# Attention mix on one core: 172 instead of 158 blocks on VectorE, earlier score products for them, the reciprocal product on GpSimd, and other costs in the list

## The chip, the core and the metric

The kernel runs on one core of a Trainium2 chip. The metric is the device time of one execution in microseconds. The core has five engines with instruction streams of their own: TensorE (PE; its weight loads are PEld in the profile), VectorE (DVE), ScalarE (ACT), GpSimd (POOL) and SyncE (SP), which issues the DMAs here. Each executes its instructions in the order written; they wait for each other through semaphores.

## What is computed

Two attention blocks read the same input x (2048 rows, 512 wide, 32 heads of 16). A is full attention over all 2048 keys, B a dilated window of 8 keys two rows apart. A gate mixes the two.

```
g = sigmoid((x * gate_w).sum(-1))
A: p = softmax(q k^T / 4) over 2048 keys;       a = (p v) @ A_wo
B: p = softmax(q . k[s - 2w], w = 0..7);        b = (p v) @ B_wo
out = g * a + (1 - g) * b
```

## The kernel before

**Periods and blocks.** Queries are cut into four chunks of 512. A period `pi` is one chunk with a group of four heads (32 periods, L320); its scores are 16 key tiles of 128 x 4 heads = 64 blocks of 128 x 512. Of every period's blocks, `n_dve[pi]` go to VectorE and the others to ScalarE.

**Blocks on ScalarE.** Blocks are taken in sets of 3 and 2 in turn. For a set, PE makes the score products into one of two PSUM rings (`qk`, L896: one 32-row strip a head, so that products of different heads run together), ScalarE takes the exponential of the whole set into `pT` (`ex`, L902), and PE adds its products with v to the period's accumulator `acc` (`pv`, L924: one 32-column strip a head).

**Blocks on VectorE.** For such a block PE makes an offset product and a score product into a misc bank (`dq`, L964), VectorE computes the exponential as a polynomial in four passes over 128 x 512 (`p1` to `p4`, L971 to L985; tiles `dt` and `pd`), and PE adds it to `acc` (`pv` of `d_group`, L994), for two blocks at a time.

**End of a period.** VectorE transposes `acc` into `accT` (`po1`), takes the reciprocal of the denominators into `rden` and multiplies by it into `ott` (`po2`, L1027), and after two periods transposes `ott` into `oat` (`po3`, L1034). When a chunk is complete, PE multiplies `oat` by the output weights (`wop`), and adds branch B's part (`bwo`).

**Branch B.** Its projections are on PE; its logits, softmax and weighted sums are on GpSimd, tile by tile of 128 rows, in halves of four window places (`logits_half`, L751; `av_half`, L800), with loads of shifted rows by SyncE.

**What sets the order.** Every piece of work is an `Op` (L104) with an engine, a cost `occ`, a latency `lat`, a due time `dl`, and the buffers it takes. `list_schedule` (L128) plans all of them: among the ops that can start about now on an engine it takes the one that is due first. The result is written out as one fixed order for each engine, and the instructions are chained in it (L262). The costs and due times are numbers in the source, so changing one moves instructions on all engines. An op that reads what GpSimd made is planned `slack` later than GpSimd's planned end (L215).

**Filler.** PE's planned work in the last 3.41 us (`SPAN`) is summed; where it is below the share `cover`, the list puts matmuls with a zero weight ahead of the next op (L184 to L199). `zero` (L941) writes them either to a spare misc bank or, adding nothing, to the accumulator of an open period:

```
spots = [(pi, j) for (pi, j), left in todo.items() if 1 <= left < NT]
for _ in range(n if spots else 0):
    pi, j = spots[-1]
    mm(acc_tiles[pi][32 * j:32 * j + 32, :], z32[:], ones_t[:], False, False, tile_position=(0, 32 * j))
```

**PSUM.** Two rings take five of the eight banks; the other three are the misc banks, shared by accumulators, projections and the block products of VectorE.

Of the kernel before, what the change touches and what calls it, by code (L numbers as in the profile page):

```python
# [9 lines left out]
ALU = mybir.AluOpType  # L10
AX = mybir.AxisListType
FP32 = mybir.dt.float32
# [4 lines left out]

CFG = dict(
    set_sizes=(3, 2),
    n_dve=(3,) * 2 + (4,) * 14 + (6,) * 16,  # L20
    dve_tiles=2,
    p_bufs=4,
    pairs=True,
    cover=0.74,
    force=1.0,
    d_slack=2.0,
    d_lead=4.0,
    d_early=5.0,
    pd_bufs=3,
    q_bufs=3,  # L30
    shift=6.0,
    hold=0.3,
    pv_dl=2.2,
    same=2.0,
    step=2,
    early=0.25,
    a_slack=0.6,
    v_slack=0.3,
    g_slack=4.0,
    unit=0.457,  # L40
    t0=18.5,
    b_start=32.0,
    b_space=46.7,
# [4 lines left out]
DH = 16  # L48
# [70 lines left out]


LAT = dict(pe=0.25, dve=0.10, act=0.22, pool=2.5, sp=2.2)
WAVE = lambda n: 0.03 + 0.205 * n
TURN = 0.13
SPAN, COVER, ZERO = 3.41, CFG["cover"], 0.216
AHEAD = dict(pe=0.10, dve=0.12, act=0.25, pool=0.5, sp=0.0)

# [96 lines left out]
def kernel(  # L223
# [12 lines left out]
    cfg = CFG  # L236
# [7 lines left out]
    TPC = QW // 128  # L244
    NBG = S // 32
    BPC = QW // 32
# [4 lines left out]
    work = ctx.enter_context(tc.tile_pool(name="work", bufs=2))  # L251
# [18 lines left out]
    def chain(bi):  # L270
        return chain_on("pe", bi)
# [13 lines left out]
    V = Chained(nc.vector, "dve")  # L285
    A = Chained(nc.scalar, "act")
    G = Chained(nc.gpsimd, "pool")
    SP = Chained(nc.sync, "sp")

    def mm(out, lhsT, rhs, start, stop, **kw):  # L290
        return chain(nc.tensor.matmul(out, lhsT=lhsT, rhs=rhs, start=start, stop=stop, **kw))  # L291

    def mm_ct(out, lhsT, rhs, start, stop):
# [10 lines left out]
    def op(eng, occ, fn, dl, **kw):  # L304
        o = Op(eng, occ, fn, dl, **kw)
        ops.append(o)
        return o
# [13 lines left out]
    NP = len(periods)  # L321
# [5 lines left out]
    n_dve = cfg["n_dve"]  # L327
# [8 lines left out]
    while u < len(units):  # L336
        n = SZ[len(sets) % 2]
# [31 lines left out]
    ott2 = const.tile([128, 2, BPC, 32], BF16, name="ott2")  # L369
# [106 lines left out]
    for sc in range(NC):  # L476
        st = {}
        halves = []
        for half in range(2):
            tag = ("rA", "rB")[half]  # L480
# [34 lines left out]
    o_kc = {}  # L515
    o_selk, o_kc0 = {}, []
# [80 lines left out]
    for h0, h1, pn in ((4, 8, 2), (8, 16, 4), (16, 24, 8), (24, 32, 12)):  # L597
        TB = 512 // ((h1 - h0) * DH)
        for tb in range(0, NT, TB):
            late = tb + TB > NT - NTD  # L600
# [6 lines left out]
    qt_tiles, o_q, q_tok, last_q = {}, {}, {}, [None]  # L607
# [36 lines left out]
    for sc in range(NC):  # L644
        st = {}
# [14 lines left out]
        dl = 32.0 + 2 * sc  # L660
        a = op("pe", 0.9, zc, dl, deps=[o_bw] + o_xt[sc], alloc=[tk], rel=T0 + 4.0)
# [22 lines left out]
    a = op("act", 0.25, zsig, 43.0, deps=[a], use=[tzp])  # L684
# [8 lines left out]
    def b_tile(t):  # L693
# [106 lines left out]
        def av_half(hf):  # L800
# [23 lines left out]
                    if hf:  # L824
                        G.tensor_tensor(out=st["obb"][:, cs], in0=ob[:, cs], in1=prod[:, 0, cs], op=ALU.add)
            return s
        l0 = op("pool", 10.2, logits_half(0), tb + 8, deps=[lk, qa], alloc=[tlg], use=[tks, tqb], name=f"lg{t}")
        l1 = op("pool", 10.2, logits_half(1), tb + 18, deps=[l0], use=[tks, tqb, tlg])
        a = op("dve", 0.45, sm_pre, tb + 19, deps=[l1], use=[tlg])
        a = op("pool", 0.75, sm_sub, tb + 19, deps=[a], use=[tlg], lat=0.9, slack=4.0)  # L830
        a = op("act", 0.45, sm_exp, tb + 18, deps=[a], use=[tlg])
        a = op("dve", 0.85, sm_post, tb + 21, deps=[a], use=[tlg])
        a = op("pool", 0.75, sm_div, tb + 21, deps=[a], use=[tlg], lat=0.9, slack=0.3)
        a0 = op("pool", 9.3, av_half(0), tb + 40, deps=[a, lv], alloc=[tob], use=[tlg, tvs])
        a1 = op("pool", 10.6, av_half(1), tb + 48, deps=[a0], alloc=[tbb], use=[tlg, tvs, tob])
        tk = tok("misc", NB)
        if cb not in obt_tok:
            obt_tok[cb] = tok("obt", 2)
# [47 lines left out]
    for k, us in enumerate(sets):  # L886
        st = {}
        ring = "rA" if k % 2 == 0 else "rB"
        maxn = SZ[k % 2]
        n = len(us)  # L890
        tr_ = tok(ring, 1)
        tp = tok("pT" + ring, cfg["p_bufs"])
        tn = T0 + UNIT * sum(SZ) * (k // 2) + (UNIT * SZ[0] if k % 2 else 0)
        pis = sorted(set(u_[0] for u_ in us))

        def qk(us=us, st=st, ring=ring, maxn=maxn):  # L896
            st["r"] = ps.tile([128, maxn, QW], FP32, tag=ring, bufs=1, name="ring")
            for s_, (pi, t, j) in enumerate(us):
                mm(st["r"][:, s_, :], kt_all[32 * j:32 * j + 32, periods[pi][1], t * 128:(t + 1) * 128],
                   qt_tiles[pi][32 * j:32 * j + 32, :], True, True, tile_position=(32 * j, 0))  # L900

        def ex(us=us, st=st, ring=ring, maxn=maxn, n=n):  # L902
            st["p"] = work.tile([128, maxn, QW], BF16, name="pT", tag="pT" + ring, bufs=cfg["p_bufs"])
            A.activation(out=st["p"][:, 0:n, :], in_=st["r"][:, 0:n, :], func=ACT.Exp, scale=LN2 / BITS)
        kd = [(o_kc[periods[pi][1]] if periods[pi][1] else o_kc0)[t // TPC] for pi, t, j in us]
        a = op("pe", 0.20 + 0.025 * (n - 1), qk, tn - 3.0, rows=True, deps=[o_q[pi] for pi in pis] + kd,
               alloc=[tr_], use=[q_tok[pi] for pi in pis], lat=0.47, after=[last_qk[0]], name=f"qk{k}")
        last_qk[0] = a
        b = op("act", 0.08 + 0.427 * n, ex, tn, deps=[a], alloc=[tp], use=[tr_], name=f"ex{k}")
        pend.append((us, st, tp, b))  # L910
        if cfg["pairs"] and len(pend) < 2 and k + 1 < len(sets):
            continue
        members, pend = pend, []
        for pi in sorted(set(u_[0] for m_ in members for u_ in m_[0])):
            mine = [(m_, s_, t, j) for m_ in members for s_, (p_, t, j) in enumerate(m_[0]) if p_ == pi]
            while mine:
                wave = {}
                for x in mine:
                    wave.setdefault(x[3], x)
                wave = list(wave.values())  # L920
                mine = [x for x in mine if x not in wave]
                from_ = [m_ for m_ in members if any(x[0] is m_ for x in wave)]

                def pv(pi=pi, wave=wave):  # L924
                    for m_, s_, t, j in wave:
                        pv_mm(pi, t, j, m_[1]["p"][:, s_, :], vp_all[:, t])
                first = pi not in o_first
                o = op("pe", 0.205 + 0.015 * len(wave), pv, tn + cfg["pv_dl"],
                       deps=[m_[3] for m_ in from_] + [o_v[(4 * periods[pi][1] + j, t)] for _, _, t, j in wave]
                       + ([] if first else [o_first[pi]]),  # L930
                       alloc=[acc_tok[pi], acc_two[pi]] if first else [],
                       use=[m_[2] for m_ in from_] + ([] if first else [acc_tok[pi], acc_two[pi]]), name=f"pv{k}",
                       sums=[((pi, x[3]), 1, NT) for x in wave])
                if first:
                    o_first[pi] = o
                o_pv[pi].append(o)
                if t_first[pi] < 4:
                    t_first[pi] += sum(1 for _, _, t, j in wave if t == 0)
                    o_t0[pi] = o

    def zero(n, spare):  # L941
        if spare:
            bank[0] = spare.bank
            zp = misc_ps([128, QW])
            for _ in range(n):
                mm(zp[0:32, :], z32[:], ones_t[:], True, True, tile_position=(0, 0))
            return
        spots = [(pi, j) for (pi, j), left in todo.items() if 1 <= left < NT]
        for _ in range(n if spots else 0):
            pi, j = spots[-1]  # L950
            mm(acc_tiles[pi][32 * j:32 * j + 32, :], z32[:], ones_t[:], False, False, tile_position=(0, 32 * j))

    d_last = [None]
# [1 line left out]
    def d_group(pi, gr, lo, hi):  # L955
# [5 lines left out]
        def chain_of(q_, t, j, dl):  # L961
# [20 lines left out]
            def p4():  # L982
                if q_ == 0:
                    st["pd"] = work.tile([128, 2, QW], BF16, name="pd", tag="pd", bufs=cfg["pd_bufs"])
                V.tensor_tensor(out=st["pd"][:, q_, :].bitcast(U16), in0=st["x"][:], in1=st["dt"][:], op=ALU.add)  # L985
            a = op("pe", 0.41, dq, dl - 3.8, rows=True, deps=[o_q[pi], o_kc[i][t // TPC] if i else o_kc0[t // TPC]],
                   after=[d_last[0]], alloc=[tx], use=[q_tok[pi]], rel=lo, lat=0.68, name=f"dq{pi}")
            a = op("dve", 0.70, p1, dl - 2.3, deps=[a], alloc=[td], use=[tx])
            a = op("dve", 0.70, p2, dl - 1.4, deps=[a], use=[td, tx])
# [14 lines left out]
    for pi in range(NP):  # L1004
        gs = [dorder[u_:min(u_ + 2, n_dve[pi])] for u_ in range(0, n_dve[pi], 2)]
        plen = S0[pi + 1] - S0[pi]
        for m, gr in enumerate(gs):
            d0 = S0[pi] - shift(pi)
            d_group(pi, gr, d0 - cfg["d_lead"], d0 + 2.5 + (plen - cfg["d_early"]) * (m + 1) / len(gs))


    oat_tiles, oat_tok, ott_tok, o_oat, o_ott = {}, {}, {}, {}, {}
    for pi, (c_, i) in enumerate(periods):
# [11 lines left out]
            V.transpose(out=st["a"][:].rearrange("p b d -> p (b d)"), in_=acc_tiles[pi][:])  # L1025

        def po2(c_=c_, i=i, st=st):  # L1027
            rden = work.tile([128, BPC], FP32, name="rden", tag="rden", bufs=2)
            V.reciprocal(out=rden[:], in_=st["a"][:, :, DH:DH + 1].rearrange("p b o -> p (b o)"))
            rd_bc = _ap(rden[:], [list(rden[:].ap[0]), [1, BPC], [0, DH]])  # L1030
            g0 = DH * (i % 2)
            V.tensor_tensor(out=ott2[:, c_ % 2, :, g0:g0 + DH], in0=st["a"][:, :, 0:DH], in1=rd_bc, op=ALU.mult)

        def po3(pi=pi, c_=c_, i=i):  # L1034
            if c_ not in oat_tiles:
                oat_tiles[c_] = work.tile([128, NG // 2, QW], BF16, name="oat", tag="oat", bufs=2)
            V.transpose(out=oat_tiles[c_][:, i // 2, :], in_=ott2[:, c_ % 2].rearrange("p b d -> p (b d)"))
        a = op("dve", 0.75, po1, E - 1.0, deps=o_pv[pi], alloc=[ta], use=[acc_tok[pi], acc_two[pi]], slack=cfg["a_slack"])
        o_ott[c_, i] = op("dve", 0.90, po2, E + 4.0, deps=[a], alloc=[to] if i % 2 == 0 else [], use=[ta] + ([to] if i % 2 else []))
        if i % 2:  # L1040
            o_oat[c_, i] = op("dve", 0.74, po3, E + 6.0, deps=[o_ott[c_, i], o_ott[c_, i - 1]] + ([o_oat[c_, i - 2]] if i > 1 else []),
                           alloc=[oat_tok[c_]] if i == 1 else [], use=[to] + ([oat_tok[c_]] if i > 1 else []))
# [122 lines left out]
```

## Time and profile before

| | us |
|---|---|
| runs | 898.36, 899.66, 899.74 (median 899.66) |
| profiled execution | 898.22, span 896.4 |
| first exponential pT starts, last ends | 18.6, 887.6 |
| ScalarE busy | 869.3 |
| PE busy | 788.9 |
| VectorE busy | 679.1 |
| GpSimd busy | 605.9 |
| mean granted clock of PE | 0.981 |

In the rows of the profile, L282 is the helper through which VectorE, ScalarE, GpSimd and SyncE instructions are recorded, and L291 that of the matmuls, so that the tiles' names tell the groups apart: `pT<-ring` are the exponentials, `ring<-qt,kt_all` the score products of ScalarE's blocks, `misc<-ones_t,off` and `misc<-qt,kt_all` the two of a VectorE block, `acc<-pT,vp_all` and `acc<-pd,vp_all` the sums with v, `acc<-ones_t,z` the filler. A row of windows gives, for a stretch from A to B, its length, then busy time and number of instructions of PE, PEld, VectorE, ScalarE and GpSimd, then the granted clock as a share of full speed. Busy times of PE overlap with its pipeline; a matmul of 512 columns shows some 0.38 us, but the next can start earlier.

### The profile page before, as it was taken

The numbers are of one execution on the slowest core, as the hardware profiler recorded it, in microseconds if no ns is written. First come the engines' busy times: TensorE is split into PE (matmuls) and PEld (weight loads), VectorE is DVE, ScalarE is ACT, GpSimd is POOL, SyncE is SP. The second block draws the span as 40 slices with busy tenths as digits, with TensorE's granted clock in tenths as the row PEclk, the third lists the DMA queues.
The fourth block names the chain that finished last, engine by engine and source line by source line (L and its number), as shares of the span: only waits on it lengthen the run. The fifth ranks groups of instructions, "written<-read, shape, count | busy, mean of one in ns | idle before, by whom it ended". The sixth has DMA issues, their size and how long they took to land.

```text
span 896.4 us, 18567 instructions
## 1 busy us (share of the span) xinstructions
PE 788.9 (88%) x7487; PEld 259.5 (29%) x7487; DVE 679.1 (76%) x1095; ACT 869.3 (97%) x782; POOL 605.9 (68%) x577
## 2 busy tenths in 40 slices
PE   9989998888888888898888988988888888889896
PEld 4223332223322233222222322222222222222221
DVE  6567667776768786768578888787879887788875
ACT  5999999999999999999999999999999999999996
POOL 4357849595959895969984597979798977700000
PEclk9999999999999999999999999799999999999978
DMA  9303011111030303020311211030230301000001
GB/s 278 113 2 106 2 61 48 59 48 60 2 106 2 106 2 106 7 101 2 96 36 60 71 48 60 13 95 15 92 107 3 105 1 48 1 1 1 1 13 36
DMA packets 43998, 47.37 MB, mean 53 GB/s; under 512 B 1876, under 2 KB 41348, under 8 KB 43912
## 3 DMA queue, kind: packets, MB, share of 16 engines
q1 hardware_dynamic: 43912, 46.19, 16.0%
q8 instruction: 58, 0.95, 0.4%
q14 instruction: 28, 0.23, 0.1%
HBM read 39.86 MB, written 6.33 MB: 52 GB/s over the span
## 4 chain that ended last, share of the span: by engine, by line
ACT 65%; issue 22%; PE 9%; DVE 1%; POOL 1%; DMA 1%; ACTq 0%; SPq 0%; DVEq 0%
ACT pT L282 64%; PE ring L291 3%; PE acc L291 3%; PE misc_ps L291 2%; ACT lg L282 1%; PE misc L291 1%; POOL prod L282 1%; DMA xld<-in_A_x_dram 1%; PE pxt L487 0%; DVE dt L282 0%; ACTq L1160 0%; DVE kmax_all L282 0%; SPq L282 0%; DVE osb L282 0%; DVE qt L282 0%
## 5 line engine op out<-in xcount | busy, mean ns | idle before, releaser
L282 ACT ACTIVATE pT<-ring 128x1536 bf16<-128x1536 f32 x756 | 860.4, 1420 | 9.7 <-PE ring L291 6.3
L291 PE MATMUL ring<-qt,kt_all 32*128 32x512 bf16 x1890 | 301.5, 385 | 98.2 <-ACT pT L282 92.6
L291 PE MATMUL acc<-pT,vp_all 128*17 128x512 bf16 (+1 forms) x1890 | 260.1, 389 | 0.8 <-DVE vp_all L282 0.5
L282 POOL TENSOR_TENSOR prod<-prod 128x512 f32<-128x512 f32 (+1 forms) x208 | 241.3, 1173 | 6.3
L291 PEld LDWEIGHTS <-kt_all 32*128 32x128 bf16 x2048 | 124.1, 91 | 389.5 <-issue 373.0
L282 POOL TENSOR_TENSOR prod<-ksh,qb 128x512 f32<-128x512 bf16 x128 | 144.5, 1161 | 50.3 <-DMA ksh<-kv_scr 30.9
L282 DVE TENSOR_SCALAR dt<-misc 128x512 f32<-128x512 uint16 x158 | 108.5, 687 | 70.5 <-PE misc L291 68.1
L282 POOL TENSOR_TENSOR prod<-vsh,lg 128x512 f32<-128x512 bf16 x128 | 137.9, 1109 | 2.5
L282 DVE SCALAR_TENSOR_TENSOR dt<-misc,dt 128x512 f32<-128x512 uint16 x158 | 108.8, 688 | 4.6
L282 DVE TENSOR_TENSOR dt<-misc,dt 128x512 f32<-128x512 uint16 x158 | 108.7, 688 | 4.6
L282 DVE TENSOR_TENSOR pd<-misc,dt 128x512 uint16<-128x512 f32 x158 | 108.6, 687 | 4.4
L291 PEld LDWEIGHTS <-vp_all 128*17 128x17 bf16 (+1 forms) x2048 | 55.9, 88 | 127.0 <-issue 115.9
L291 PE MATMUL acc<-ones_t,z 128*32 128x512 bf16 x233 | 85.4, 394 | 0.0
L291 PE MATMUL misc_ps<-xT,wtw 128*32 128x512 bf16 x1024 | 85.4, 383 | 0.0
L291 PE MATMUL misc_ps<-bw,xT 128*32 128x512 bf16 x768 | 66.1, 390 | 0.0
L291 PE MATMUL misc<-ones_t,off 32*128 32x512 bf16 x158 | 60.8, 385 | 0.4 <-DVE accT L282 0.3
L291 PE MATMUL misc<-qt,kt_all 32*128 32x512 bf16 x158 | 60.1, 380 | 0.0
L282 POOL TENSOR_TENSOR lg<-lg,rr 128x256 f32<-128x256 f32 x16 | 10.1, 629 | 57.0 <-DVE rr L282 40.5
L282 POOL TENSOR_TENSOR lg<-lg,mx 128x256 f32<-128x256 f32 x16 | 10.3, 644 | 49.0 <-DVE mx L282 49.0
L291 PEld LDWEIGHTS <-xT 128*32 128x32 bf16 (+1 forms) x1088 | 32.0, 96 | 27.7 <-issue 20.2
L282 DVE TENSOR_SCALAR misc_ps<-misc_ps,magn 128x512 uint32<-128x512 uint32 x32 | 24.1, 754 | 15.2 <-PE misc_ps L291 14.9
L291 PE MATMUL acc<-pd,vp_all 128*17 128x512 bf16 x158 | 34.2, 391 | 0.0
(72 smaller groups left out, 499.0 us busy)
## 6 DMA issues: line engine op xcount, KB each, us to landing
ksh<-kv_scr SPq DMA_DIRECT2D x16, 1024.0 KB, 5.7
vsh<-kv_scr SPq DMA_DIRECT2D x16, 1024.0 KB, 6.1
kv_scr<-kvs SPq DMA_DIRECT2D x16, 256.0 KB, 2.0
xld<-in_A_x_dram SPq DMA_DIRECT2D x4, 512.0 KB, 7.6
out_dram<-osb SPq DMA_DIRECT2D x16, 128.0 KB, 1.7
bw<-in_B_wqkv_dram SPq DMA_DIRECT2D x1, 1536.0 KB
wraw<-in_A_wqkv_dram SPq DMA_DIRECT2D x2, 512.0 KB, 8.7
wv<-in_A_wqkv_dram SPq DMA_DIRECT2D x1, 512.0 KB, 9.0
```

The source lines that it names most:

```text
L282: return chain_on(key, f(*a, **k))
L291: return chain(nc.tensor.matmul(out, lhsT=lhsT, rhs=rhs, start=start, stop=stop, **kw))
```

## The change

Fourteen periods (2 to 15) get 5 instead of 4 blocks on VectorE. `dq` is due 10 us earlier, and the block sums of every period but the last 8 us later (`d_late`). The product with the reciprocal becomes an op of its own on GpSimd, except in the last two periods. The filler goes, where it can, to the column strip of the matmul before it. `cover` falls from 0.74 to 0.68, and the list's costs for PE, ScalarE and GpSimd are replaced; `first` is 0 and has no effect.

```diff
-    n_dve=(3,) * 2 + (4,) * 14 + (6,) * 16,
+    n_dve=(3,) * 2 + (5,) * 14 + (6,) * 16,
-    cover=0.74,
+    cover=0.68,
+    dq_early=10.0,
+    d_late=8.0,
+    first=0.0,
-    unit=0.457,
+    unit=0.461,
...
-WAVE = lambda n: 0.03 + 0.205 * n
-TURN = 0.13
+WAVE = lambda n: 0.01 + 0.205 * n
+TURN = 0.10
...
     def mm(out, lhsT, rhs, start, stop, **kw):
+        strip[0] = kw.get("tile_position", (0, 0))[1] // 32
...
-        l0 = op("pool", 10.2, logits_half(0), ...
-        l1 = op("pool", 10.2, logits_half(1), ...
+        l0 = op("pool", 9.6, logits_half(0), ...
+        l1 = op("pool", 9.6, logits_half(1), ...
...
-        a0 = op("pool", 9.3, av_half(0), ...
-        a1 = op("pool", 10.6, av_half(1), ...
+        a0 = op("pool", 8.8, av_half(0), ...
+        a1 = op("pool", 10.0, av_half(1), ...
...
-        a = op("pe", 0.20 + 0.025 * (n - 1), qk, ...
+        a = op("pe", 0.21 + 0.003 * (n - 1), qk, ...
-        b = op("act", 0.08 + 0.427 * n, ex, ...
+        b = op("act", 0.047 + 0.432 * n, ex, ...
-                o = op("pe", 0.205 + 0.015 * len(wave), pv, tn + cfg["pv_dl"],
+                o = op("pe", 0.207 + 0.003 * len(wave), pv, tn + cfg["pv_dl"] - (cfg["first"] if first else 0.0),
...
-            pi, j = spots[-1]
+            pi, j = max(spots, key=lambda x: (x[1] == strip[0], x[0]))
...
-            a = op("pe", 0.41, dq, dl - 3.8, ...
+            a = op("pe", 0.43, dq, dl - 3.8 - cfg["dq_early"], ...
...
-            d_group(pi, gr, d0 - cfg["d_lead"], d0 + 2.5 + (plen - cfg["d_early"]) * (m + 1) / len(gs))
+            late = cfg["d_late"] if pi < NP - 1 else 0.0
+            d_group(pi, gr, d0 - cfg["d_lead"], d0 + 2.5 + late + (plen - cfg["d_early"]) * (m + 1) / len(gs))
...
+        def po2m(pi=pi, c_=c_, i=i, st=st):
...
+            (V if pi >= NP - 2 else G).tensor_tensor(out=ott2[:, c_ % 2, :, g0:g0 + DH], in0=st["a"][:, :, 0:DH], in1=rd_bc, op=ALU.mult)
...
-        o_ott[c_, i] = op("dve", 0.90, po2, E + 4.0, ...
+        a = op("dve", 0.26, po2, E + 0.2, deps=[a], use=[ta])
+        if pi >= NP - 2:
+            o_ott[c_, i] = op("dve", 0.45, po2m, E + 0.3, ...
+        else:
+            o_ott[c_, i] = op("pool", 0.75, po2m, E + 1.5, deps=[a], lat=0.95, slack=2.0, ...
```

More of the change, by code (lines that the diff above doesn't have):

```diff
@@ L288 @@
     SP = Chained(nc.sync, "sp")
+    strip = [0]
     def mm(out, lhsT, rhs, start, stop, **kw):
+        strip[0] = kw.get("tile_position", (0, 0))[1] // 32
         return chain(nc.tensor.matmul(out, lhsT=lhsT, rhs=rhs, start=start, stop=stop, **kw))
@@ L826, in av_half @@
             return s
-        l0 = op("pool", 10.2, logits_half(0), tb + 8, deps=[lk, qa], alloc=[tlg], use=[tks, tqb], name=f"lg{t}")
-        l1 = op("pool", 10.2, logits_half(1), tb + 18, deps=[l0], use=[tks, tqb, tlg])
+        l0 = op("pool", 9.6, logits_half(0), tb + 8, deps=[lk, qa], alloc=[tlg], use=[tks, tqb], name=f"lg{t}")
+        l1 = op("pool", 9.6, logits_half(1), tb + 18, deps=[l0], use=[tks, tqb, tlg])
         a = op("dve", 0.45, sm_pre, tb + 19, deps=[l1], use=[tlg])
@@ L833, in b_tile @@
         a = op("pool", 0.75, sm_div, tb + 21, deps=[a], use=[tlg], lat=0.9, slack=0.3)
-        a0 = op("pool", 9.3, av_half(0), tb + 40, deps=[a, lv], alloc=[tob], use=[tlg, tvs])
-        a1 = op("pool", 10.6, av_half(1), tb + 48, deps=[a0], alloc=[tbb], use=[tlg, tvs, tob])
+        a0 = op("pool", 8.8, av_half(0), tb + 40, deps=[a, lv], alloc=[tob], use=[tlg, tvs])
+        a1 = op("pool", 10.0, av_half(1), tb + 48, deps=[a0], alloc=[tbb], use=[tlg, tvs, tob])
         tk = tok("misc", NB)
@@ L905 @@
         kd = [(o_kc[periods[pi][1]] if periods[pi][1] else o_kc0)[t // TPC] for pi, t, j in us]
-        a = op("pe", 0.20 + 0.025 * (n - 1), qk, tn - 3.0, rows=True, deps=[o_q[pi] for pi in pis] + kd,
+        a = op("pe", 0.21 + 0.003 * (n - 1), qk, tn - 3.0, rows=True, deps=[o_q[pi] for pi in pis] + kd,
                alloc=[tr_], use=[q_tok[pi] for pi in pis], lat=0.47, after=[last_qk[0]], name=f"qk{k}")
         last_qk[0] = a
-        b = op("act", 0.08 + 0.427 * n, ex, tn, deps=[a], alloc=[tp], use=[tr_], name=f"ex{k}")
+        b = op("act", 0.047 + 0.432 * n, ex, tn, deps=[a], alloc=[tp], use=[tr_], name=f"ex{k}")
         pend.append((us, st, tp, b))
@@ L985, in p4 @@
                 V.tensor_tensor(out=st["pd"][:, q_, :].bitcast(U16), in0=st["x"][:], in1=st["dt"][:], op=ALU.add)
-            a = op("pe", 0.41, dq, dl - 3.8, rows=True, deps=[o_q[pi], o_kc[i][t // TPC] if i else o_kc0[t // TPC]],
+            a = op("pe", 0.43, dq, dl - 3.8 - cfg["dq_early"], rows=True, deps=[o_q[pi], o_kc[i][t // TPC] if i else o_kc0[t // TPC]],
                    after=[d_last[0]], alloc=[tx], use=[q_tok[pi]], rel=lo, lat=0.68, name=f"dq{pi}")
@@ L1027, in po2 @@
         def po2(c_=c_, i=i, st=st):
-            rden = work.tile([128, BPC], FP32, name="rden", tag="rden", bufs=2)
-            V.reciprocal(out=rden[:], in_=st["a"][:, :, DH:DH + 1].rearrange("p b o -> p (b o)"))
+            st["rden"] = work.tile([128, BPC], FP32, name="rden", tag="rden", bufs=2)
+            V.reciprocal(out=st["rden"][:], in_=st["a"][:, :, DH:DH + 1].rearrange("p b o -> p (b o)"))
+        def po2m(pi=pi, c_=c_, i=i, st=st):
+            rden = st["rden"]
             rd_bc = _ap(rden[:], [list(rden[:].ap[0]), [1, BPC], [0, DH]])
             g0 = DH * (i % 2)
-            V.tensor_tensor(out=ott2[:, c_ % 2, :, g0:g0 + DH], in0=st["a"][:, :, 0:DH], in1=rd_bc, op=ALU.mult)
+            (V if pi >= NP - 2 else G).tensor_tensor(out=ott2[:, c_ % 2, :, g0:g0 + DH], in0=st["a"][:, :, 0:DH], in1=rd_bc, op=ALU.mult)
         def po3(pi=pi, c_=c_, i=i):
@@ L1038 @@
         a = op("dve", 0.75, po1, E - 1.0, deps=o_pv[pi], alloc=[ta], use=[acc_tok[pi], acc_two[pi]], slack=cfg["a_slack"])
-        o_ott[c_, i] = op("dve", 0.90, po2, E + 4.0, deps=[a], alloc=[to] if i % 2 == 0 else [], use=[ta] + ([to] if i % 2 else []))
+        a = op("dve", 0.26, po2, E + 0.2, deps=[a], use=[ta])
+        if pi >= NP - 2:
+            o_ott[c_, i] = op("dve", 0.45, po2m, E + 0.3, deps=[a], alloc=[to] if i % 2 == 0 else [], use=[ta] + ([to] if i % 2 else []))
+        else:
+            o_ott[c_, i] = op("pool", 0.75, po2m, E + 1.5, deps=[a], lat=0.95, slack=2.0, alloc=[to] if i % 2 == 0 else [], use=[ta] + ([to] if i % 2 else []))
         if i % 2:
```

## The prediction

> **What bounds the kernel now.** I read the page's busy times and costliest groups first, then the waits of ScalarE, then windows around them. In the group line, "860.4, 1420" is busy time and mean of one, "9.7" the idle time before.
>
> ```profile
> PE 788.9 (88%) x7487; PEld 259.5 (29%) x7487; DVE 679.1 (76%) x1095; ACT 869.3 (97%) x782; POOL 605.9 (68%) x577
> ...
> L282 ACT ACTIVATE pT<-ring 128x1536 bf16<-128x1536 f32 x756 | 860.4, 1420 | 9.7 <-PE ring L291 6.3
> ```
>
> In the waits of ScalarE the columns are total, times and longest, in us:
>
> ```profile
> ACT pT L282 <- PE ring L291: 6.3, 10, 1.7
> ACT pT L282 <- PE acc L291: 2.8, 3, 1.1
> ACT pT L282 <- PE misc L291: 0.4, 1, 0.4
> ```
>
> ScalarE's exponentials are the clock of this kernel: 860.4 us of the 896.4 us span, and the chain of waits gives ACT 65%. The first starts at 18.6 us, the last ends at 887.6 us; between them ScalarE stops for 9.5 us less the 1.7 us before the first, so 7.8 us. All of it is waiting for TensorE (PE). The windows tell the two kinds apart (length, then busy PE, PEld, DVE, ACT, POOL, then the granted clock):
>
> ```profile
> 491.80:495.20 3.40, 3.05 (x34) 1.03 (x33) 3.18 (x6) 2.53 (x3) 0.10 (x1) 1.00 0.20 77
> 565.82:569.23 3.41, 2.18 (x20) 0.71 (x20) 3.27 (x7) 3.41 (x4) 3.33 (x4) 1.00 0.02 5
> 569.23:579.47 10.24, 10.24 (x60) 1.84 (x58) 7.27 (x12) 8.27 (x8) 10.08 (x10) 0.50 0.00 0
> 620.43:623.85 3.42, 2.55 (x21) 0.87 (x19) 3.35 (x8) 3.42 (x5) 3.42 (x4) 1.00 0.00 0
> 859.37:862.78 3.41, 2.58 (x18) 0.97 (x18) 3.27 (x7) 3.41 (x5) 0.00 (x0) 1.00 0.00 0
> 862.78:873.02 10.24, 10.24 (x54) 2.01 (x53) 6.76 (x11) 8.75 (x8) 0.00 (x0) 0.50 0.04 14
> 541.90:545.30 3.40, 2.42 (x22) 0.75 (x18) 3.30 (x7) 3.40 (x4) 0.00 (x0) 1.00 0.75 255
> ```
>
> First kind: four stretches (from 569, 624, 709 and 863 us; 10.24, 3.41, 3.41 and 10.24 us long) with the granted clock at 0.50. PE is then busy throughout and ScalarE starves. They hold the waits for "ring" other than the first and the one for "misc": 6.3 - 1.7 + 0.4 = 5.0 us. Each follows a stretch of 3.41 us in which PE was busy for only 2.2 to 2.6 us; 542 us shows that not every such stretch (2.42 us) brings one. Second kind: three stops at full clock (494.0, 502.1, 814.0 us; 0.87, 0.87, 1.09 us), together the 2.8 us for "acc", where the list put too much other PE work between two score sets.
>
> **Part by part.**
>
> *Fourteen blocks leave ScalarE.* n_dve sums to 2x3 + 14x4 + 16x6 = 158 before and 2x3 + 14x5 + 16x6 = 172 after, so ScalarE gets 1876 blocks instead of 1890, in 751 exponentials instead of 756. At 860.4 / 1890 = 0.455 us a block that is 14 x 0.455 = **6.4 us off the engine that bounds**. Nothing hides ScalarE's time, so it comes off whole.
>
> *VectorE takes them.* Each costs four passes of 0.688 us: 14 x 4 x 0.688 = +38.5 us. The reciprocal product leaves it in 30 of 32 periods:
>
> ```profile
> L282 DVE TENSOR_TENSOR ott<-accT,rden x32: 424/566/1423, 55.2 to 889.1; 128x256 bf16<-128x256 f32 x32
> ```
>
> ```profile
> 300.00:500.00 200.00, 177.07 (x1773) 59.36 (x1769) 146.47 (x231) 199.13 (x180) 153.43 (x146) 1.00 0.18 58
> 500.00:700.00 200.00, 175.35 (x1563) 53.67 (x1561) 167.36 (x262) 196.52 (x178) 174.66 (x165) 0.97 0.18 56
> ```
>
> The first row is minimum, median and maximum in ns; the windows' third busy time is VectorE's. The group's 22.8 us less two of 0.425 at the end makes -21.9 us. The additional blocks all lie in periods 2 to 15, about 74 to 458 us. There VectorE is 146.5 / 200 = 73% busy; 38.5 us over 384 add 10 points, the products leaving (about 13 of 0.88 us) take 3 off: 80%. From 500 to 700 us it already runs at 84% with six blocks a period, and every ScalarE stop there is accounted for above without it. So I cost VectorE at nothing; the cover is this idle fifth, and without it each late block sum holds PE's queue, and the score sets behind it.
>
> *The product on GpSimd* is not in the trace. Nearest row: its 128x256 product lg<-lg,rr, 0.629 us; 30 x 0.63 = 19 us on an engine with 290 us idle, which ends its own work at about 784 us: nothing on the path. A far bound is its slowest single step, 1.5 us, which still makes only 45 us. What can cost is the wait: its reader on VectorE, the oat transpose (L1037), and all block passes queued behind that. In the built order the transpose stands 2 to 23 VectorE instructions after the reciprocal, as against 2 to 5 before, so mostly past the product's time. I take 0; the high bound is rival 3.
>
> *Score products ahead of the passes* (due times 10 us earlier) change when dq is issued on PE, not its cost, 0.43 us. VectorE waits 68.1 us for this product now, 81 times; less of that makes the 80% easier. An earlier dq holds one of three misc banks longer; PE's waits for VectorE at these tiles are 0.5 us in all today. I take 0.
>
> *Filler matmuls.* The list uses 211 after, 240 before. What matters is whether they add PE time:
>
> ```profile
> 492.27 0.39 PE L291 MATMUL acc<-ones_t,z 128*32 128x512 bf16 x1
> 492.28 0.39 PE L291 MATMUL acc<-pd,vp_all 128*17 128x512 bf16 x2
> 492.50 0.38 PE L291 MATMUL acc<-ones_t,z 128*32 128x512 bf16 x1
> ```
>
> The first filler shares its time with the block sums, which start 10 ns later; the second starts 220 ns after. Before, 76 of the 240 stand right behind a matmul of another column strip and so can run beside it; after, since the strip of the last matmul is preferred, 5 of 211. Fillers that add time go from 164 to 206. With 14 x 0.43 us more block products, the streaming time of all matmuls counted from the order (0.216 us a step, different strips together; both as the starts above are apart) rises from 558 to 573 us. Stretches of three score sets (about 3.4 us, as long as those above) with less than half of streaming fall from 13 to 8. I scale the half-clock cost by that: 5.0 x 8/13 = 3.1, so **-1.9 us**. Bounds: -5.0 (no drop left) and +5.0 (twice as many, if the lower count of fillers decides).
>
> The Trainium skill, "TensorE: Matmul & The Clock Gate", section "HAM oscillation — how this bites in real kernels", says that the clock halves after PE-idle gaps above some 3.4 us. This trace disagrees: the half clock follows stretches with PE busy for 2.2 to 2.6 of 3.41 us. By that rule the fillers decide nothing, and the sum would be that of rival 1.
>
> *New crowding.* Full-clock stops appear in the order before: PE work between two score sets (priced under rival 2) exceeds ScalarE's 1.13 us by 1.03, 0.81 and 1.23 us at the three places (stops 0.87, 0.87, 1.09), while three lone excesses of 0.8 cost nothing. The order after has one big excess, 2.3 us, near set 412: eight bwo products, two of dq, nine sums, sixteen wop products, five sums in a row. I price it at 2.3 and its neighbour of 0.8 at 0.5: 2.8, as before, so 0. Bounds -0.8 (the big one alone, reduced by the ring's lead to 2.0) and +1.
>
> **Sum:** -6.4 - 1.9 + 0 = -8.3 us. The profiled execution took 898.2 us (span 896.4 and 1.8 around it), so it would be 889.9; it lies 1.4 us under the median 899.66, to which I apply the sum: **891.4 us**. Own range: -6.4 - 5.0 - 0.8 to -6.4 + 1, or 887.5 to 894.3 (to 899.3 with drops doubled).
>
> **Rivals.**
>
> 1. *Fillers don't matter, the drops stay.* For: 542 us had a stretch as thin as the others without a drop; the drops depend on where stretches fall. Only ScalarE's share counts: 899.66 - 6.4 = 893.3 us.
>
> 2. *Crowding on PE eats the gain.* PE work in the order (the streaming steps and 0.10 us for each change between row and column tiling, as score set to sum starts 0.31 us apart) rises by 13.5 us (703 to 716.5) against a shorter ScalarE time; stretches of two score sets with more PE than ScalarE work go from 55 to 81. Against: most of the 55 cost nothing. If each of the 26 costs 0.25 us, 6.5 us return: 897.9 us, about no change.
>
> 3. *Slower: VectorE blocked behind the GpSimd product.* GpSimd runs in order, and half a logits tile is 4 x 1.16 + 3 x 1.27 + 0.61 + 0.43 = 9.5 us in one piece. A product that arrives inside one waits 4.8 us on average. At six of the 15 transposes fed by GpSimd only 3 to 6 VectorE instructions (about 3 us of cover) lie between; the rest, 1.8 us, stops the passes. If no lead of the passes over the sums absorbs it, PE and ScalarE stop as long: 6 x 1.8 = 10.8 us, giving 902.2 us. It decides from 8.3 / 6 = 1.4 us for each. Against: VectorE never waited noticeably for GpSimd at mx<-lg (0.0 us idle before it), which the same list places; and planned halves (9.6 us) are no shorter than the measured 9.5.
>
> **Numbers.** Forecast 0.57, rival 1 0.22, rival 2 0.08, rival 3 0.13. About 0.2% (1.8 us) can be told from no change. Faster: the first two and a third of rival 2, 0.81; within 0.2%: 0.06; slower 0.13. The range runs from 886.5 (all drops gone and stops at full clock shrunk) to 899.5 us, which leaves out rival 3 and little else.
>
> **What would show it.** ScalarE's pT group at about 854 us in 751; VectorE busy near 696, GpSimd near 625. Right: few or short half-clock slices, one ScalarE stop of 2 us near 470 us, none on VectorE's account. Wrong: half-clock time above the present 27 us, waits of VectorE's oat for GpSimd with PE's acc waits behind them, or many small ring waits at full clock.

## The result, and the profile after

| | before | changed |
|---|---|---|
| median of four runs, us | 899.13 | 890.01 (888.93 to 891.62) |
| ratio | | 0.9901, interval 0.9883 to 0.9918 |
| profiled execution, us (span) | 898.22 (896.4) | 891.62 (889.8) |

The kernel is 9.1 us faster at the median; 8.3 was forecast, to 891.4 us. Beside the experiments below the changed kernel was timed once more: 890.01 against 897.38 (ratio 0.9926, interval 0.9897 to 0.9954). The medians in this document leave out five runs counted as slow (a_oldstrip 904.6 and 907.4 us, a_dveprod 901.9 and 1094.6, g_h02_c71 902.3; the one of 1094.6 us had a mean granted clock of 0.552), and with them these three medians are 893.6, 891.0 and 888.3. The page of the changed kernel, busy times and two groups:

```profile
PE 800.3 (90%) x7472; PEld 261.5 (29%) x7472; DVE 696.3 (78%) x1121; ACT 862.7 (97%) x777; POOL 619.3 (70%) x607
...
L285 ACT ACTIVATE pT<-ring 128x1536 bf16<-128x1536 f32 x751 | 853.8, 1411 | 8.6 <-PE ring L297 6.3
...
L285 POOL TENSOR_TENSOR ott<-accT,rden 128x256 bf16<-128x256 f32 x30 | 18.7, 622 | 76.2 <-DVE rden L285 76.2
```

L285 and L297 are the helpers that were L282 and L291. The exponentials take 6.6 us less, VectorE stands at 696.3 us, and the product costs GpSimd 0.622 us each. The 76.2 us before the product are GpSimd's wait for the reciprocal, not a wait of others for GpSimd. ScalarE's waits in the same execution (total, times, longest):

```profile
ACT pT L285 <- PE ring L297: 6.3, 7, 1.7
ACT pT L285 <- PE acc L297: 1.9, 1, 1.9
...
ACT e L285 <- PE misc_ps L679: 0.5, 1, 0.5
```

The one wait of 1.9 us for "acc" is the crowded place that the order showed, here in the timeline (start, length, engine, instruction):

```profile
487.67 0.39 PE L297 MATMUL ring<-qt,kt_all 32*128 32x512 bf16 x3 [0.25 <-ACT pT L285]
...
488.90 0.61 PE L297 MATMUL misc_ps<-bwo,obt 128*32 128x512 bf16 x8
...
489.45 0.39 PE L297 MATMUL misc<-ones_t,off 32*128 32x512 bf16 x1
...
489.68 0.37 PE L297 MATMUL misc<-qt,kt_all 32*128 32x512 bf16 x1
...
489.98 0.82 PE L297 MATMUL acc<-pT,vp_all 128*32 128x512 bf16 x9
...
490.48 1.19 PE L297 MATMUL misc_ps<-wop,oat 128*32 128x512 bf16 x16
490.48 2.36 ACT L285 ACTIVATE pT<-ring 128x1536 bf16<-128x1536 f32 x2 [1.95 <-PE acc L297]
...
491.35 0.59 PE L297 MATMUL acc<-pT,vp_all 128*17 128x512 bf16 x5
...
491.98 0.39 PE L297 MATMUL ring<-qt,kt_all 32*128 32x512 bf16 x3
```

The score set that this exponential reads was ready at 488.1 us (its products start at 487.67). What ScalarE waits for is the nine sums: they read older pT tiles, of which each ring has four buffers (`p_bufs`), and an exponential can't write until one is free. Counting the instructions of the trace bears this out: at 489.9 us ScalarE has finished 410 score sets, and PE the sums of 402 of them and one of the next. Eight sets are outstanding, as many as the two rings have buffers. The list had put sixteen bwo products and two of dq ahead of these sums. So this is the place that the order showed, but the link is the pT buffer and not, as the prediction has it, a late score set. The stops at 494, 502 and 814 us before read the same way: "acc", ended by sums that start 0.49, 0.50 and 0.50 us earlier, with eight sets outstanding each time. Two of the three:

```profile
494.38 0.40 PE L291 MATMUL acc<-pT,vp_all 128*17 128x512 bf16 x4
...
494.87 1.45 ACT L282 ACTIVATE pT<-ring 128x1536 bf16<-128x1536 f32 x1 [0.87 <-PE acc L291]
...
814.63 0.62 PE L291 MATMUL acc<-pT,vp_all 128*32 128x512 bf16 x8
...
815.13 1.45 ACT L282 ACTIVATE pT<-ring 128x1536 bf16<-128x1536 f32 x1 [1.09 <-PE acc L291]
```

Half clock, that is, stretches with a granted clock of 0.50, stands in these windows (length, PE, PEld, VectorE, ScalarE, GpSimd, clock; the last two numbers are of the DMA); two of these stretches are left before the last exponential, 17 us instead of 27:

```profile
318.82:322.23 3.41, 1.95 (x20) 0.71 (x20) 3.22 (x9) 3.41 (x5) 3.24 (x4) 1.00 0.00 0
322.23:325.64 3.41, 3.41 (x26) 0.75 (x19) 1.57 (x3) 2.58 (x3) 3.27 (x5) 0.50 0.00 0
830.82:834.23 3.41, 2.39 (x22) 0.86 (x21) 2.64 (x5) 3.41 (x5) 0.00 (x0) 1.00 0.00 0
834.23:847.88 13.65, 13.65 (x59) 2.61 (x58) 8.51 (x13) 10.72 (x10) 0.00 (x0) 0.50 0.00 0
```

Again each follows a thin stretch (PE busy for 1.95 and 2.39 of 3.41 us). The stops of ScalarE in and just after them add up to 0.83 + 3.00 = 3.8 us, 5.0 before.

One stop is new:

```profile
40.95 0.68 DVE L285 COPY zrow<-misc_ps 1x512 f32<-1x512 f32 x1 [1.25 <-DMA z_scr<-zrow]
...
41.68 1.02 PE L297 MATMUL misc_ps<-xT,gw 128*1 128x512 bf16 x4 [0.65 <-DVE zrow L285]
...
43.13 4.62 ACT L285 ACTIVATE pT<-ring 128x1536 bf16<-128x1536 f32 x4 [0.91 <-PE ring L297]
```

The gate's rows go out through the two accT buffers. The third waits for the first one's DMA, which in the chain of waits takes 5.6 us from 35.3 us, right behind the issue of the 1 MB load vsh (32.6 us). PE waits for that row with the score sets behind it; ScalarE loses 0.9 us, and 0.5 us more at the gate's exponential.

The difference of the two spans by part (changed less before; gaps of ScalarE of over 0.1 us counted as stops): first exponential 0.8 us later; ScalarE's work without stops 854.5 against 861.2, -6.7; stops at full clock 3.5 against 2.8, +0.6; stops with half clock -1.2; the end -0.2. Sum -6.6, which is 889.8 less 896.4. The rest to 9.1 is where the two profiled executions lie: 1.6 us above the median of the changed kernel, where this one is the slowest of four, and 0.9 us under that of before. Much of how runs of one kernel differ goes with the clock: over 85 runs of the kernel before, each us of half clock goes with 0.23 us of time (a straight line through time and granted clock; times 893.0 to 903.7). The length of half clock is (1 - clock) x 2 x span; it includes the 4 to 6 us of it after the last exponential (9 us without fillers), which ScalarE doesn't feel.

### The profile page after: what moved, and what is told of

Same layout as the page of the kernel before. It is cut to its first block, busy times and chain, and to the rows that moved or that the text cites. A ratio compares the mean times of both kernels' runs of the same rounds, so it can differ in the third digit from the quotient of the medians.

```text
span 889.8 us, 18611 instructions
## 1 busy us (share of the span) xinstructions
PE 800.3 (90%) x7472; PEld 261.5 (29%) x7472; DVE 696.3 (78%) x1121; ACT 862.7 (97%) x777; POOL 619.3 (70%) x607
## 4 chain that ended last, share of the span: by engine, by line
ACT 65%; issue 25%; PE 6%; DMA 2%; DVE 1%; SPq 0%; DVEq 0%; ACTq 0%
ACT pT L285 65%; PE ring L297 2%; PE misc_ps L297 2%; PE acc L297 2%; ACT lg L285 1%; DMA xld<-in_A_x_dram 1%; DMA z_scr<-zrow 1%; PE misc L297 0%; DMA zrows<-z_scr 0%; PE pxt L493 0%; DVE zrow L285 0%; DVE osb L285 0%; SPq L285 0%; DVE qt L285 0%; DVE misc_ps L285 0%
## 5 line engine op out<-in xcount | busy, mean ns | idle before, releaser
L285 ACT ACTIVATE pT<-ring 128x1536 bf16<-128x1536 f32 x751 | 853.8, 1411 | 8.6 <-PE ring L297 6.3
L297 PE MATMUL ring<-qt,kt_all 32*128 32x512 bf16 x1876 | 298.6, 383 | 77.2 <-ACT pT L285 71.2
L285 POOL TENSOR_TENSOR prod<-prod 128x512 f32<-128x512 f32 (+1 forms) x208 | 240.1, 1168 | 6.3
L297 PE MATMUL acc<-pT,vp_all 128*17 128x512 bf16 (+1 forms) x1876 | 242.0, 386 | 0.2
L297 PEld LDWEIGHTS <-kt_all 32*128 32x128 bf16 x2048 | 123.6, 91 | 366.6 <-issue 349.8
L285 DVE TENSOR_SCALAR dt<-misc 128x512 f32<-128x512 uint16 x172 | 117.6, 684 | 75.5 <-PE misc L297 72.0
L285 POOL TENSOR_TENSOR prod<-ksh,qb 128x512 f32<-128x512 bf16 x128 | 144.0, 1159 | 30.5 <-DMA ksh<-kv_scr 18.8
L285 POOL TENSOR_TENSOR prod<-vsh,lg 128x512 f32<-128x512 bf16 x128 | 136.6, 1100 | 4.3 <-DMA vsh<-kv_scr 2.3
L285 DVE TENSOR_TENSOR dt<-misc,dt 128x512 f32<-128x512 uint16 x172 | 118.3, 688 | 5.0
L285 DVE TENSOR_TENSOR pd<-misc,dt 128x512 uint16<-128x512 f32 x172 | 118.2, 687 | 5.1
L285 DVE SCALAR_TENSOR_TENSOR dt<-misc,dt 128x512 f32<-128x512 uint16 x172 | 118.2, 687 | 4.9
L297 PEld LDWEIGHTS <-vp_all 128*17 128x17 bf16 (+1 forms) x2048 | 52.0, 88 | 124.8 <-issue 116.9
L297 PE MATMUL misc_ps<-xT,wtw 128*32 128x512 bf16 x1024 | 86.8, 386 | 0.0
L297 PE MATMUL acc<-ones_t,z 128*32 128x512 bf16 x206 | 71.7, 390 | 0.0
L285 POOL TENSOR_TENSOR ott<-accT,rden 128x256 bf16<-128x256 f32 x30 | 18.7, 622 | 76.2 <-DVE rden L285 76.2
L297 PE MATMUL misc_ps<-bw,xT 128*32 128x512 bf16 x768 | 66.2, 382 | 0.0
L297 PE MATMUL misc<-ones_t,off 32*128 32x512 bf16 x172 | 65.7, 382 | 0.4 <-DVE pd L285 0.4
L297 PE MATMUL misc<-qt,kt_all 32*128 32x512 bf16 x172 | 64.8, 377 | 0.0
L297 PEld LDWEIGHTS <-xT 128*32 128x32 bf16 (+1 forms) x1088 | 34.8, 96 | 29.8 <-issue 19.4
L297 PE MATMUL acc<-pd,vp_all 128*17 128x512 bf16 x172 | 40.1, 384 | 0.0
L285 POOL TENSOR_TENSOR lg<-lg,mx 128x256 f32<-128x256 f32 x16 | 10.1, 632 | 40.4 <-DVE mx L285 40.4
L285 POOL TENSOR_TENSOR lg<-lg,rr 128x256 f32<-128x256 f32 x16 | 10.1, 631 | 35.6 <-ACT pT L285 19.2
```

Source lines behind the costliest of these rows:

```text
L285: return chain_on(key, f(*a, **k))
```

## The experiments

Labels that begin with a_ are the changed kernel with one edit, those with b_ the kernel before with one edit, and after_again is the changed kernel itself; p_u457_c70, g_h02_c71 and p_158 are the versions under "A better order". The ratio is to runs of the kernel before taken beside each (medians 896.2 to 897.4). "Half clock" is the median length worked out as above; the kernel before has 25 us (median of the 85 runs), the changed one 19.5. The texts written before each run speak of an excess, PE work between two score sets beyond ScalarE's 1.13 us, and of thin stretches, three score sets of which less than half is streaming. Both are the author's counts in the order as built; no view of the profile shows them.

| kernel | us | ratio to before, interval | half clock, us |
|---|---|---|---|
| after_again | 890.0 | 0.9926, 0.9897 to 0.9954 | 19.5 |
| b_newstrip | 895.3 | 0.9992, 0.9971 to 1.0014 | 16.1 |
| a_oldstrip | 892.8 | 0.9947, 0.9920 to 0.9975 | 33.9 |
| a_nofill | 935.0 | 1.0417, 1.0377 to 1.0456 | 252 |
| b_172 | 903.7 | 1.0084, 1.0057 to 1.0111 | 43.3 |
| a_158 | 892.6 | 0.9967, 0.9942 to 0.9991 | 17.8 |
| a_oldcosts | 893.2 | 0.9958, 0.9937 to 0.9979 | 17.8 |
| a_dveprod | 890.5 | 0.9930, 0.9903 to 0.9958 | 28.4 |
| a_dqlate | 889.4 | 0.9924, 0.9893 to 0.9954 | 10.7 |
| p_u457_c70 | 883.8 | 0.9854, 0.9828 to 0.9881 | 10.6 |
| g_h02_c71 | 888.2 | 0.9922, 0.9886 to 0.9958 | 23.0 |
| p_158 | 891.1 | 0.9945, 0.9922 to 0.9967 | 10.7 |

### The changed kernel once more

> The changed kernel once more, beside the others on one chip. Theory: 0.99 of the kernel before, which on this kind of chip means 888 beside 897; its clock share above that with the old filler strip (median 0.980).

890.0 beside 897.4. Its profile is an execution without half clock before the last exponential, so it shows the kernel's other stops alone (view of the cores, then waits of ScalarE):

```profile
core 0: 885.2 us, clock 0.996
```

```profile
ACT pT L285 <- PE ring L297: 3.1, 2, 1.7
ACT pT L285 <- PE acc L297: 1.9, 1, 1.9
```

Besides the 1.7 us at the start only the crowded place (1.9 us) and the gate (1.4 + 0.4 us) are left: 3.7 us to be won by a better order.

### Do fillers hold the clock up?

```diff
-    cover=0.68,
+    cover=0.0,
```

> The changed kernel without filler matmuls in the main part (cover 0). 100 thin stretches of three sets instead of 8. Theory (thin stretches bring the half clock): half-clock time of 100 us or more instead of some 17, at about 0.22 us each, so 15 to 45 us slower than the changed kernel. Rival (by a rule of idle gaps above 3.4 us, of which there are none here): clock as before or better, within 1 us.

45 us slower, at the upper end of the expectation. The page's clock row, a window, and ScalarE's waits:

```profile
PEclk9999999989999998997798987867879566999655
```

```profile
549.23:552.65 3.42, 1.93 (x18) 0.58 (x15) 2.60 (x5) 3.42 (x5) 1.07 (x2) 1.00 0.56 172
552.65:569.71 17.06, 16.33 (x94) 3.38 (x93) 11.69 (x18) 13.63 (x12) 16.21 (x16) 0.50 0.24 82
```

```profile
ACT pT L285 <- PE ring L297: 35.7, 57, 1.7
ACT pT L285 <- PE misc L297: 4.6, 10, 0.9
```

ScalarE stops 57 times for score sets instead of 7. The longest idle time between two matmuls from 20 to 870 us is 0.95 us here and also 0.95 us in the changed kernel, so no idle gap of 3.4 us is involved, and without fillers half clock grows from 19.5 to 252 us. That refutes the thought of rival 1 that fillers decide nothing. The rule of the Trainium skill ("TensorE: Matmul & The Clock Gate", section "HAM oscillation — how this bites in real kernels"), no idle gaps above some 3.4 us, does not describe this kernel: no trace of any run has a gap above 1.58 us between the first and the last exponential, and the clock halves all the same.

What goes with half clock is how little PE is busy in a stretch. The granted clock changes in steps of 3.41 us. Cut into these steps, the fourteen traces have 3396 at full clock between the first and the last exponential. After all 8 in which PE was busy for less than 2.1 us the clock was halved, after 41 of the 471 with 2.1 to 2.81 us, and after none of the 2917 with more. So half clock came only after a thin step, but in the middle range most thin steps brought none; what decides there is open.

For the strip of the filler alone, both ways:

```diff
-            pi, j = spots[-1]
+            pi, j = max(spots, key=lambda x: (x[1] == strip[0], x[0]))
```

> The kernel before with one edit: filler goes, where it can, to the column strip of the matmul before it (10 of 241 fillers stand behind another column strip, 76 without the edit). The planned order is otherwise the same, ScalarE's blocks stay 1890. Theory (fillers that add PE time keep the clock up): half-clock stretches shorter than the 27 us of before, cost down from 5.0 to about 3 us, so about 2 us faster: 897. Rival (fillers decide nothing, as by a rule of idle gaps above 3.4 us): 899, with half-clock stretches as before.

> The changed kernel with the filler in the strip as before (56 of 212 stand behind another column strip, 5 with the edit); order otherwise the same. Theory: stretches of three score sets with under half of streaming 12 instead of 8, half-clock cost up by about 2 us: 892. Rival (fillers decide nothing): 890.

In the kernel before, the new strip shortens half clock from 25 to 16 us and brings the median from 897.0 to 895.3, nearly the 2 us expected; but two of its twelve runs are at 902, and the interval of the ratio includes 1. In the changed kernel the old strip lengthens it from 19.5 to 34 us and costs 2.8 us at the median, with an interval that overlaps that of the changed kernel. Time at 0.23 us for each us of half clock would be -2.1 and +3.3. So the direction and size fit, both times, and neither is established by its time alone: that the strip is worth about 2 us stays an estimate.

### Do the blocks pay alone?

```diff
-    n_dve=(3,) * 2 + (4,) * 14 + (6,) * 16,
+    n_dve=(3,) * 2 + (5,) * 14 + (6,) * 16,
```

> The kernel before with 5 instead of 4 blocks a period in periods 2 to 15, nothing else. Theory (ScalarE bounds, VectorE has room even with the reciprocal products on it): 6.4 us off, of which more crowding in the order (one excess of 1.9 us, five of 1.0, where before has 1.2, 1.0 and 0.8) gives some 2 back: 893 to 896. Rival (VectorE must be relieved for the blocks to pay): block sums late, waits of PE for VectorE, 899 or more.

They do not: 0.84% slower, outside the 893 to 896 of the theory. ScalarE's waits and two windows of VectorE:

```profile
ACT pT L282 <- PE acc L291: 9.0, 8, 1.8
ACT pT L282 <- PE ring L291: 4.0, 3, 1.7
ACT pT L282 <- PE misc L291: 1.1, 1, 1.1
```

```profile
100.00:300.00 200.00, 178.10 (x1738) 61.47 (x1729) 162.77 (x261) 196.15 (x177) 145.15 (x138) 1.00 0.15 49
300.00:500.00 200.00, 181.70 (x1806) 60.08 (x1806) 161.22 (x256) 197.40 (x178) 162.09 (x154) 1.00 0.16 53
```

The time is in the rival's range, but its reason, VectorE late, shows in the profile at one place only: a stop of 1.1 us at 56 us, before which PE waited 1.6 us for VectorE's transpose of an accumulator. VectorE is 81% busy (third busy time), and ScalarE waits for crowds of PE work, 9.0 us in eight stops where the kernel before has 2.8 in three. In this execution ScalarE's own work is 6.0 us shorter, as it should be, but its stops at full clock are 10.2 us instead of 2.8, so crowding takes back more than the blocks give. My price for the order's excesses was too low: five of the eight stops are of 0.86 or 0.87 us, where I had allowed some 2 us for all six places together. To that comes half clock, 43 us at the median; this execution, the fastest of six, has 10 us of it before the last exponential. Why the list with its old numbers crowds PE so much more with 172 blocks I did not follow further.

The reverse, the new list with 158 blocks:

> The changed kernel with 158 blocks on VectorE as before, so 1890 on ScalarE; its order has no excess above 0.8 us between two score sets. Theory: ScalarE 6.4 us longer, the stop of 1.9 us at full clock gone: 890.0 + 6.4 - 1.9 = 894.5. Rival (the gain comes from the new costs and due times of the list, not from ScalarE's share): 890 or less.

892.6, 2.6 us above the changed kernel where 4.5 was expected; against the runs beside each, -4.4 and -7.4, so 3.0. Its profile has 1.6 us of stops at full clock where the second profile of the changed kernel has 3.9 (gaps of over 0.1 us counted), so the difference should be 6.4 - 2.3 = 4.1; about 1 us stays open. So with equal blocks the new list, strip and product together are already worth some 4 us, and the fourteen blocks, with the crowded stop that comes with them, some 3.

### Which part of the rest?

```diff
-WAVE = lambda n: 0.01 + 0.205 * n
-TURN = 0.10
+WAVE = lambda n: 0.03 + 0.205 * n
+TURN = 0.13
...
-        b = op("act", 0.047 + 0.432 * n, ex, ...
+        b = op("act", 0.08 + 0.427 * n, ex, ...
```

With it go the old costs of qk, pv and dq, unit 0.457 and cover 0.74. GpSimd's costs stay the new ones.

> The changed kernel with the list's old costs for TensorE and ScalarE, the old unit and cover 0.74. Its order has four excesses above 1.2 us (1.7, 1.5, 1.2, 1.2) and ten thin stretches. Theory (stops at full clock come out at about the excess less 0.2): stops of 5 us instead of 1.9, so 3 us slower than the changed kernel. Rival (the costs matter little, blocks and filler strip do it): within 1 us of the changed kernel.

3.2 us slower, as expected: its profile has 6.3 us of waits for "acc" in five stops instead of 1.9 in one. Half clock is no longer than the changed kernel's at the median (17.8 against 19.5 us), so it is the crowding.

```diff
-            (V if pi >= NP - 2 else G).tensor_tensor(out=ott2[:, c_ % 2, :, g0:g0 + DH], ...
+            V.tensor_tensor(out=ott2[:, c_ % 2, :, g0:g0 + DH], ...
...
-        if pi >= NP - 2:
+        if True:
```

> The changed kernel with the reciprocal product back on VectorE in all periods. Its order then has no excess above 0.8 us between two score sets (2.3 with the product on GpSimd), 182 fillers for 212 and 13 thin stretches of three sets for 8. Theory (VectorE has room, the product's place is worth little by itself): within 2 us of the changed kernel, its stop of 1.9 us near 488 us gone, more half clock instead. Rival (the blocks pay only because the product left VectorE): block sums late, 3 us or more slower than the changed kernel.

890.5: within 1 us of the changed kernel, with intervals that nearly coincide. The crowded stop is gone (none of over 0.4 us for "acc" in its profile) and half clock is 28 us instead of 19.5, some 2 us of time at 0.23 each; the two cancel about. The product's place on GpSimd is not what makes the change fast.

```diff
-    dq_early=10.0,
-    d_late=8.0,
+    dq_early=0.0,
+    d_late=0.0,
```

> The changed kernel with the score products and block sums of VectorE's blocks due as before (dq_early and d_late 0). Order: excesses 1.0 and 0.8, 9 thin stretches. Theory (VectorE has room either way): its waits for TensorE's product rise above 72 us, the time is that of the changed kernel less its crowding stop plus up to 1, 888 to 891. Rival (the early products keep the passes on time): block sums late, 893 or more.

889.4, the same as the changed kernel. VectorE's waits for the score products are 77 us with 72 in the changed kernel, so earlier products hardly shorten them, and block sums come in time either way. Both due times were set back at once, so neither is tested alone.

### A better order

Two versions that take away the stops that the profile of the changed kernel shows: due times of the gate from 32 to 44 us to 90 to 150 us; and unit, hold and cover so that the order has no excess above 0.8 us. The first keeps the product on VectorE; its edits:

```diff
-    cover=0.68,
-    unit=0.461,
+    cover=0.70,
+    unit=0.457,
...
-        dl = 32.0 + 2 * sc
+        dl = 90.0 + 12 * sc
...
+            V.tensor_tensor(out=ott2[:, c_ % 2, :, g0:g0 + DH], ...
```

> A version that should beat both: 172 blocks, product on VectorE, due times of the gate moved from 32 to 44 us to 90 to 150 us, unit 0.457, cover 0.70. Its order has no excess above 0.8 us between two score sets, 314 fillers and 5 thin stretches (8 in the changed kernel). Theory: stops of the gate at 42 to 48 us (1.4 us) and of the crowding (1.9 us) gone, half-clock time not above that of the changed kernel: 886 to 887. Rival (100 more fillers crowd TensorE, each delaying a score set): 890 or more.

> Another such version with the product on GpSimd: gate's due times as there, hold 0.2, cover 0.71; no excess above 0.8, 319 fillers, 9 thin stretches. Theory: 887, some half clock more than the version with 5 thin stretches. Rival: as there, 890 or more. If the product's place matters for VectorE, this one is the faster of the two by 2 us or more.

The first is 883.8, 1.46% under the kernel before, and better than expected. Its ScalarE waits, where 1.7 of the 3.2 us are the start:

```profile
ACT pT L285 <- PE ring L297: 3.2, 3, 1.7
```

No stop for "acc" and none at the gate are left, the rest is one stretch of half clock (6.8 us, at 822 us). Of the 6.2 us between the medians of this version and the changed kernel, the two stops make 1.9 + 1.4 and half clock, 10.6 us instead of 19.5, some 2.0 at 0.23 each. The edits were made together, so which of them brings what is not shown. The second is 888.2: fast in its least disturbed runs (885.9), but with 23 us of half clock at the median. Nine thin stretches against five: the 319 and 314 fillers are as many, they only stand elsewhere. That the second isn't faster says once more that the product needn't leave VectorE.

The same first version with 158 blocks prices the blocks without a crowded place on either side:

> The best version so far (172 blocks, product on VectorE, no stop by crowding) with 158 blocks on VectorE; its order has one lone excess of 0.9 us and 8 thin stretches instead of 5. It isolates the price of the fourteen blocks where neither order has a crowding stop. Theory (each block is worth ScalarE's 0.455 us, nothing else): 883.8 + 6.4 = 890.2, up to 1 more for thin stretches. Rival (the blocks are worth half of it, as the changed kernel with 158 blocks, 2.6 us above the changed kernel, might suggest): 887.

891.1 against 883.8 is 7.2 us for fourteen blocks (8.1 against the runs of before beside each), with equal half clock (10.7 and 10.6 us): 0.52 us each or more by the medians. The rows of the exponentials in the two profiled executions differ by 6.4 us:

```profile
L285 ACT ACTIVATE pT<-ring 128x1536 bf16<-128x1536 f32 x756 | 859.4, 1436 | 2.8 <-PE ring L297 2.6
L285 ACT ACTIVATE pT<-ring 128x1536 bf16<-128x1536 f32 x751 | 853.0, 1432 | 3.4 <-PE ring L297 3.2
```

The spans, 889.1 and 883.0 us, differ by 6.1. So the blocks are worth ScalarE's 0.455 us each, and not half of it; the other 0.8 us of the medians stays open.

## Why the prediction was right

- *ScalarE bounds, and fourteen blocks are 6.4 us.* Held: -6.6 us in the row of the exponentials, and in the clean pair 6.4 us in that row and 7.2 us of time. But they pay in full only in an order without new crowds: alone, in the old list, they made the kernel slower, and in the changed kernel taking them back costs only 2.6 to 3.0 us, as the crowded stop goes with them.
- *VectorE takes them behind its idle fifth.* Held: 161.0 and 152.1 us busy of 200 in the windows from 100 and 300 us, and PE's waits for block passes are 0.4 us in all. The forecast of 80% for periods 2 to 15 was about right.
- *The product on GpSimd costs nothing.* Held: 0.622 us against 0.63 assumed (the bound of 1.5 us for GpSimd's slowest step overlooks the set-up, where one takes 2.15 us), and no VectorE wait for an oat transpose. One wait of 1.0 us, at an accT transpose, is put down to GpSimd, but the last sums that this transpose reads end right before it too (641.72 us, start 641.84). Rival 3 falls; so does the thought that this move makes room that the blocks need (a_dveprod).
- *Early score products.* Costed at nothing, and worth nothing that can be told (a_dqlate).
- *Fillers, -1.9 us.* That fillers hold the clock up was shown (a_nofill); that the new strip does was not established by time. The size came out nearly: -1.2 in the profiled executions, and 25 to 19.5 us of half clock at the medians, 1.3 us at 0.23 each. Scaling by counted thin stretches (8/13) was a rough guess, and that it came out close is in part luck.
- *Crowding, 0.* One stop of 1.95 us where 2.0 to 2.3 was read from the order (at 489 us, where 470 was named), its neighbour cost nothing: 0.9 less than before. The step that failed is the link: ScalarE waited for sums that free a pT tile, not for a score set. Reading excesses in the order was right for one big place; for several of about 1.0 the price was too low (b_172).
- *What was missed:* the stop at the gate, +1.4 us. I read the moved instructions for the edited operations only; the new numbers also moved the gate's, which no edit names.

The profiled executions differ by 6.6 us, the medians by 9.1 and 7.4 in the two comparisons; 8.3 lies among them. The main term is shown; that the sum came so near is in part luck. The errors (+1.4 at the gate, +0.7 for fillers, -0.9 for crowding, +0.8 for a first exponential that started later) partly cancel, and are no larger than what the clock changes from run to run.

## What to carry to other kernels

Where one engine is saturated, work taken off it is worth its row's time only if the queue that feeds it doesn't get a new crowd: count, in the order as built, the feeder's work between two feeds and ahead of what frees the consumer's buffers, and compare it with the consumer's time. (More pT buffers, which would loosen that link, weren't tried.) A filler that runs beside another matmul adds no streaming time; here half clock followed only steps of 3.41 us with PE busy for 2.81 us or less. And when a planner's numbers change, look also at the operations that no edit names.

## What was not expected of the hardware

TensorE's clock halved after steps of 3.41 us in which PE was busy for 1.4 to 2.8 us, with no idle gap above 1.58 us between the first and last exponential of any trace (0.95 or less in eight of the fourteen), in lengths of 3.41 us and multiples of it, up to 37.5 us (a_dveprod) and, without fillers, 63 us at the end. Without fillers the granted clock stood at a mean of 0.858. The same kernel's time varied by 10.7 us over 85 runs (893.0 to 903.7), with the granted clock.

VectorE's product of two SBUF operands took 0.424 us at its fastest and 1.423 at its slowest in the kernel before. The nine of its 32 instances with no GpSimd product beside them took 0.424 to 0.426 us, the other 23 from 0.425 to 1.423. Each of the 20 that were slower than 0.43 us ended 0.26 to 0.29 us after the end of the GpSimd instruction that was running when it started, so VectorE seems to wait that one out. On GpSimd the same product took 0.618 to 0.628 us throughout, and GpSimd's other work fell by 5 us with the move: from 605.9 us to 619.3 less 18.7 = 600.6, and with the product back on VectorE it is 605.7 (a_dveprod).
